# A recurrence followed by two gated MLPs: the two fp16 copies of each unit move from ScalarE to VectorE after the first four chunks

## Chip, cores and metric

The kernel runs on one core of one Trainium2 chip. The metric is the device time of one execution in microseconds (us); lower is better. Engine names are those of the profile: PE is TensorE (PEld its weight loads), DVE is VectorE, ACT is ScalarE, POOL is GpSimd, SP is SyncE, which here only issues DMAs.

## What is computed

The inputs of the recurrence have shape 4 x 8 x 768 x 40 (batch, heads, sequence, head size). Each of the 32 batch-head pairs carries a 40 x 40 state through 768 steps, and the output of a step is read before the state is updated. The 3072 x 320 result goes through two MLPs, the second of them gated.

```python
for t in range(S):
    y[:, :, t] = einsum('bhd,bhde->bhe', rt, state)
    Sa = einsum('bhde,bhe->bhd', state, at)
    state = state * wt[:, :, None, :] - einsum('bhd,bhe->bhde', Sa, bt) + einsum('bhd,bhe->bhde', vt, kt)
h = x @ w_in                      # 320 -> 2048
g = where(h >= 1, h, where(h <= -1, 0, (h + 1)**2 / 4))
x = g @ w_out                     # 2048 -> 320
out = (silu(x @ w_gate) * (x @ w_val)) @ w_out2   # 320 -> 1536 -> 320
```

## The kernel before, in words

**Chunks and units.** The sequence is cut into 12 chunks of 64 steps. Within a chunk the steps are solved together by matrix products and one triangular inverse, so that the state passes only from chunk to chunk. A unit is one chunk of one batch entry (8 heads); there are 4 units in a chunk and 48 in all, numbered n = 4c + j. Every fp32 operand of a matmul is kept as two fp16 parts, a high part and the rest, side by side in one tile.

**Stages.** `decay_tasks` (L664) builds running products of w and their reciprocals, for four chunks at a time. `p_tasks` (L788) prepares a unit: it scales a, r, k and b, splits them (tiles `ars`, `kbs`), turns them by a DMA transpose (`art`, `kbT`) and multiplies them (`lkt`, `l21`, and L to memory). `inv_tasks` (L885) solves the triangular system of a chunk on DVE in 31 steps of two operations (L915, L920). `m_tasks` (L973) is the part of a unit that depends on the state of the chunk before. `in1`, `in2` and `outp` (L1196, L1211, L1225) are the MLPs, on 256 rows (one chunk) at a time; their matmuls are at L1170 and L1234.

**What m_tasks does with a unit.** ACT loads v scaled (L994), casts it to the fp16 tile `vh` (L1018), and POOL writes the rest to `vss` (`split`, L539). A copy at L1026 writes `vh` twice into the first 64 rows of `vss` (64 x 640 values). PE multiplies (L1038). Then, for each of two half chunks: ACT writes two fp16 copies of the result (L1062), DVE the rest (L541, called from L1066), PE multiplies by the inverse (`mm_sa`, L1048), ACT and DVE split that into rows of `vss` (L1073, L541); between the halves PE runs `mm_c` (L1054). When `vss` is full, a DMA transpose turns it (`vsT`, L771), and a second copy, at L1098, puts both fp16 parts of all 128 rows of `vss` (128 x 640 values) beside the weights of the unit's output in tile `wt`. PE multiplies `vsT` (L1106), DVE masks it (L1109), ACT and DVE split it into the other part of `wt` (L1113, L539), and PE computes output and new state (L1127). DVE and ACT then scale and split the state (L1134 to L1146), which DMAs carry to where the next chunk reads it (L1148, L1152). The last chunk has no second copy, as it makes no state.

**Which engine makes the two copies.** Line L1025 chooses an operation, an engine and a cost for both: below chunk `VO` ACT's copy, from `VO` on DVE's. `VO` is 12 before the change, so ACT makes all 48 copies of L1026 and all 44 of L1098.

**What sets the order.** Nothing is issued in the order of the source. Each piece of work is a task with an engine, a cost, the results it reads, the buffers it uses and a first priority `p`. `Plan.forward` (L64) is a list scheduler run at build time: it starts on each engine the ready task of lowest priority number, and models buffers, DMA and PE's slower clock. A task marked `lk`, and every POOL task, keeps DVE and POOL apart: it is taken to begin its work only after the last such task of the other engine. `Plan.backward` goes over the same tasks from the end and gives new priorities; `run` (L301) alternates the two up to eight times and keeps the shortest plan. On each engine the tasks are then issued in that plan's order, and on the chip each engine works through its list in order.

**First priorities.** `m0(n)` (L1268) is the due time of a unit, from `PER` (one chunk) less `LEAD`. `decay_tasks`, `p_tasks`, `inv_tasks` and `m_tasks` get `m0` less leads of their own; `BP`, `BI`, `BM` and `BD` are extra leads of chunk 0 (of its p, inv and m tasks and of the first decay group), `P1` and `M1` those of chunk 1, and `DP` sets the second half of a decay group behind the first. The MLP tasks of chunk c are due at `PER` x c and on, whatever `LEAD` is.

Of the kernel before, what the change touches and what calls it, by code (L numbers as in the profile page):

```python
# [322 lines left out]
def tile_recurrence__then__gated_mlps(  # L323
# [35 lines left out]
    ARP = range(1, 12)  # L359
    XSP = range(12)  # L360
    NH = 1
    VO = 12
    WSP = True
    NW1 = 14
    NLO = 2
# [141 lines left out]
    def c_s(n):  # L507
        return 0.08 + n * 0.86e-3
# [464 lines left out]
    def m_tasks(n, p):  # L973
# [23 lines left out]
        if j % 2 == 0:  # L997
# [26 lines left out]
          r=[(key, "vh")], w=[(key, "vl")], use=V + VH + VS, p=p - 1)  # L1024
        copy, eng, cost = (s_.copy, "ACT", c_s(2 * HD)) if c < VO else (v_.tensor_copy, "DVE", 0.24)  # L1025
        T(eng, cost, lk=eng == "DVE", emit=lambda: copy(  # L1026
# [235 lines left out]
                    out=out[r0:r0 + C, :], in_=o()[64 * q:64 * q + 64]),  # L1262
                    r=[(ok, tt, 1)], w=[("out", c)], use=[("u", uk)], p=p, dma=0.31)

    PER, LEAD, PLEAD, DLEAD, WLEAD, ILEAD, WSTEP, LPRI, LSTEP, BP, BI, BM, DP, BD, P1, M1 = 69.67, 10.07, 94.28, 203.97, -34.92, 128.76, 0.3, 29.05, 2.22, -0.71, 2.76, 0.74, 10.0, 113.83, 18.78, 5.0
    SUP = PER / B

    def m0(n):  # L1268
# [112 lines left out]
```

## Time and profile before

| what | value |
|---|---|
| median of 3 runs (range) | 1157.68 us (1153.25 to 1157.78) |
| the profiled execution's own time | 1155.31 us |
| span of its profile, first to last instruction | 1153.6 us |
| mean granted clock of TensorE, share of full speed | 0.972 |
| PE busy | 910.4 us |
| ACT busy | 866.0 us |
| DVE busy | 755.0 us |
| POOL busy | 569.0 us |

The durations in this document come from the one profiled execution; 1.7 us of its time lie outside the span. Busy time is the time in which an engine has an instruction under way. In a table by stretches each engine has its busy time and, in brackets, its number of instructions, followed by the granted clock and the DMA engines' busy share. A line "A <- B" in a table of waits is idle time of engine A ahead of an instruction, ended by B: total, number of times, longest. In a table of groups the part after the bar is busy time and mean duration, then the idle time ahead of the group's instructions and what ended it. In the view of one line or tile, durations in ns are given as smallest, median and largest, then the first and the last start.

### The profile page before, as it was taken

What the parts mean: (1) busy time and instruction counts of PE and PEld (TensorE: products, weight loads), DVE (VectorE), ACT (ScalarE), POOL (GpSimd) and SP (SyncE); (2) the same over time, 40 slices, a digit from 0 to 9 for tenths busy, and PEclk for the clock granted to TensorE, in tenths of its full rate; (3) what the DMA queues carried; (4) which work ended last, traced back from release to release, by engine and by line L of the source; (5) the groups of instructions that cost most, each with busy time, mean ns of one, the idle gap of its engine ahead of it and who ended that gap; (6) DMA issues with size and microseconds to landing.
All of it is one profiled execution on the core that took longest, in us unless ns stands there. A gap on an engine that the chain in (4) does not pass through costs nothing. (4 is left out here: it accounts for less than half of the span.)

```text
span 1153.6 us, 29900 instructions
## 1 busy us (share of the span) xinstructions
PE 910.4 (79%) x11328; PEld 745.1 (65%) x11328; DVE 755.0 (65%) x1830; ACT 866.0 (75%) x1628; POOL 569.0 (49%) x756
## 2 busy tenths in 40 slices
PE   0131246744789899989999899999999999999998
PEld 0131235533567777777777787787777777888886
DVE  7778796886879487585765856856758457442211
ACT  2595687876996998988979979788798796763422
POOL 5689634533566536545554545545545433322321
PEclk9999999766899999999999999999999999999999
DMA  9988699669979888787977877799667534321000
GB/s 212 240 200 169 182 149 159 147 116 197 195 145 152 122 124 143 134 129 126 147 121 126 134 123 128 127 134 140 103 130 129 101 75 76 60 44 32 4 15 23
DMA packets 560948, 144.63 MB, mean 125 GB/s; under 512 B 537140, under 2 KB 544820, under 8 KB 560804
## 3 DMA queue, kind: packets, MB, share of 16 engines
q1 hardware_dynamic: 523036, 135.08, 64.8%
q10 hardware_dynamic: 37768, 7.66, 4.3%
q8 instruction: 88, 1.44, 0.6%
q14 instruction: 56, 0.46, 0.2%
HBM read 74.87 MB, written 18.14 MB: 81 GB/s over the span
## 5 line engine op out<-in xcount | busy, mean ns | idle before, releaser
L539 POOL TENSOR_TENSOR mx<-mx 128x512 f16<-128x512 f32 x168 | 194.7, 1161 | 271.8 <-ACT mx L1190 252.1
L1234 PE MATMUL po<-wo,mx 128*128 128x320 f16 x2016 | 314.3, 302 | 3.9 <-DVE mx L541 2.5
L1234 PEld LDWEIGHTS <-mx 128*128 128x128 f16 x2016 | 191.1, 98 | 72.9 <-DVE mx L541 2.8
L1170 PE MATMUL ph<-mx,w 128*128 128x256 f16 x1536 | 194.0, 278 | 17.4 <-DMA mx<-x 10.1
L1170 PEld LDWEIGHTS <-w 128*128 128x128 f16 x1536 | 147.6, 99 | 41.7 <-issue 18.4
L1170 PE MATMUL ph<-x2t,wv 128*128 128x256 f16 x1152 | 141.3, 272 | 4.9 <-DVE mx L1220 3.2
L1170 PE MATMUL ph<-x2t,wg 128*128 128x256 f16 x1152 | 140.9, 273 | 2.3 <-ACT mx L1216 2.2
L1190 ACT CAST mx<-mx 128x512 f16<-128x512 f32 x168 | 102.9, 615 | 48.1 <-DVE mx L1220 30.1
L1206 DVE SCALAR_TENSOR_TENSOR mx<-ph,mx 128x512 f32<-128x512 f32 x96 | 66.2, 690 | 94.6 <-ACT mx L1203 94.2
L1170 PEld LDWEIGHTS <-wv 128*128 128x128 f16 x1152 | 110.4, 98 | 20.0 <-issue 6.5
L1170 PEld LDWEIGHTS <-wg 128*128 128x128 f16 x1152 | 109.8, 98 | 17.7 <-issue 2.9
L920 DVE TENSOR_TENSOR pg<-pg,ub 128x126 f32<-128x126 f32 (+22 forms) x372 | 96.4, 259 | 9.8
L915 DVE SCALAR_TENSOR_TENSOR ub<-ub,pg 128x126 f32<-128x126 f32 (+22 forms) x372 | 92.4, 248 | 14.5 <-DMA ub<-lsd 4.5
L1220 DVE SCALAR_TENSOR_TENSOR mx<-ph,mx 128x512 f32<-128x512 f32 x72 | 49.4, 686 | 71.9 <-PE ph L1170 69.0
L1062 ACT ACTIVATE xs<-px 32x320 f16<-32x320 f32 x176 | 75.0, 426 | 11.6 <-PE px L1054 6.1
L545 POOL TENSOR_TENSOR ldp<-ldp 128x320 f32<-128x320 f32 (+1 forms) x90 | 76.6, 864 | 11.8 <-ACT ldp L822 5.5
L1073 ACT ACTIVATE vss<-px 32x640 f16<-32x640 f32 x88 | 61.1, 695 | 12.3 <-PE px L1048 10.3
L1048 PEld LDWEIGHTS <-tt 96*32 96x32 f16 x768 | 28.5, 95 | 64.4 <-issue 45.2
L541 DVE SCALAR_TENSOR_TENSOR xs<-px,xs 32x320 f16<-32x320 f32 x88 | 42.6, 484 | 39.7 <-ACT xs L1062 37.3
L1202 ACT ACTIVATE mx<-ph 128x512 f32<-128x512 f32 x96 | 57.0, 594 | 12.6 <-PE ph L1170 10.5
L539 POOL TENSOR_TENSOR vss<-ldv,vh 128x320 f16<-128x320 f32 x48 | 38.5, 801 | 56.5 <-ACT vh L1018 25.0
L541 DVE SCALAR_TENSOR_TENSOR vss<-px,vss 32x320 f16<-32x320 f32 x88 | 43.4, 493 | 30.0 <-ACT vss L1073 24.8
(226 smaller groups left out, 1713.9 us busy)
## 6 DMA issues: line engine op xcount, KB each, us to landing
ldv<-in_v_dram SPq DMA_DIRECT2D x88, 80.0 KB
ub<-lsd SPq DMA_DIRECT2D x22, 256.0 KB
wo<-in_moe_w_out_dram SPq DMA_DIRECT2D x17, 320.0 KB
ldp<-was SPq DMA_DIRECT2D x23, 160.0 KB
out_dram<-mx SPq DMA_DIRECT2D x46, 80.0 KB
wo<-in_moe_w_in_dram SPq DMA_DIRECT2D x7, 512.0 KB
ldp<-in_b_dram SPq DMA_DIRECT2D x22, 160.0 KB
ldp<-wks SPq DMA_DIRECT2D x22, 160.0 KB
```

The source lines that it names most:

```text
L539: e.tensor_tensor(out=out, in0=x, in1=hi, op=ALU.subtract)
L541: e.scalar_tensor_tensor(out=out, in0=x, scalar=scale, in1=hi, op0=ALU.mult, op1=ALU.subtract)
L545: e.tensor_tensor(out=out, in0=x, in1=y, op=ALU.mult)
L915: v_.scalar_tensor_tensor(out=t, in0=L()[:, j, j + 1:].unsqueeze(1).to_broadcast([128, nm, ni]), scalar=-(2.0**-10), in1=m[:, 0:nm, j:j + ...
L920: v_.tensor_tensor(out=m[:, 0:nm, j + 1:], in0=m[:, 0:nm, j + 1:], in1=t, op=ALU.add)
L1062: s_.activation(out=xs[32 * i:32 * i + 32], in_=px[32 * hf:32 * hf + 32], func=AF.Copy, scale=-(2.0**-10))
L1073: s_.activation(out=hi2(G("vss", key)[z]), in_=two(hd(G("px", key))[z]), func=AF.Copy, scale=2.0**-8)
L1170: t_.matmul(out=ps, lhsT=wts[:, wi, fs], rhs=xT[:, xi, :], start=(i == 0), stop=(i == len(plan) - 1))
L1190: T("ACT", c_s(512), lambda: s_.copy(out=G("g", key)[:, 0], in_=u2(key)), r=[(key, "u")], w=[(key, "gh")], use=U + GG, p=p)
L1202: s_.activation(out=u2(key), in_=ps2(key), func=AF.Relu, scale=2.0**-8, bias=1.0)
L1206: T("DVE", c_v(512, True), lambda: v_.scalar_tensor_tensor(out=u2(key), in0=ps2(key), scalar=2.0**8, in1=u2(key), op0=ALU.max, op1=ALU.min ...
L1234: t_.matmul(out=ps, lhsT=g[:, x, f, 128 * tt:128 * tt + 128], rhs=wo[:, 2 * i + f, y, :], start=(i == 0 and f == 0 and m == 0), stop=(i == ...
```

## The change

`VO` becomes 4: the copies at L1026 and L1098 are ACT's in chunks 0 to 3 and DVE's (`tensor_copy`) in chunks 4 to 11. Each DVE copy is given a cost of 0.24 to plan with, and the mark `lk`. Six of the planner's first-priority numbers change as well: `LEAD`, `BI`, `BM`, `DP`, `BD` and `M1`.

```diff
-    VO = 12
+    VO = 4
...
-    PER, LEAD, PLEAD, DLEAD, WLEAD, ILEAD, WSTEP, LPRI, LSTEP, BP, BI, BM, DP, BD, P1, M1 = 69.67, 10.07, 94.28, 203.97, -34.92, 128.76, 0.3, 29.05, 2.22, -0.71, 2.76, 0.74, 10.0, 113.83, 18.78, 5.0
+    PER, LEAD, PLEAD, DLEAD, WLEAD, ILEAD, WSTEP, LPRI, LSTEP, BP, BI, BM, DP, BD, P1, M1 = 69.67, 13.46, 94.28, 203.97, -34.92, 128.76, 0.3, 29.05, 2.22, -0.71, -1.04, 2.57, 15.51, 135.59, 18.78, 2.07
```

## Rows read from the trace of the kernel before

**Rows 1.** The page, busy time of each engine over the span.
```profile
span 1153.6 us, 29900 instructions
PE 910.4 (79%) x11328; PEld 745.1 (65%) x11328; DVE 755.0 (65%) x1830; ACT 866.0 (75%) x1628; POOL 569.0 (49%) x756
```

**Rows 2.** Table by stretches, four stages of the span.
```profile
core 0: us, PE busy (x) PEld busy (x) DVE busy (x) ACT busy (x) POOL busy (x), PEclk, DMA share, GB/s
0.00:180.00 180.00, 41.51 (x616) 35.67 (x617) 144.76 (x399) 114.07 (x197) 124.04 (x243) 1.00 0.88 189
180.00:420.00 240.00, 175.47 (x2193) 138.06 (x2193) 180.31 (x396) 195.89 (x373) 120.30 (x144) 0.87 0.84 153
420.00:1020.00 600.00, 563.91 (x7300) 464.03 (x7300) 402.75 (x993) 507.46 (x970) 290.75 (x337) 1.00 0.72 119
1020.00:1154.00 134.00, 129.49 (x1223) 107.34 (x1222) 27.23 (x43) 48.57 (x91) 33.93 (x34) 0.99 0.11 21
```

**Rows 3.** Waits of PE, from 420 to 1020 us.
```profile
PE px L1048 <- DVE xs L541: 11.8, 15, 1.4
PE px L1054 <- DVE vss L541: 4.5, 8, 1.6
PE pg L1127 <- DVE wt L539: 4.1, 10, 1.1
PE ph L1170 <- DVE mx L1220: 2.8, 3, 1.7
PE ph L1170 <- DVE mx L1206: 2.5, 4, 1.0
PE ph L1170 <- ACT mx L1216: 2.2, 3, 0.8
PE pg L1106 <- DMA vsT<-vss: 1.2, 1, 1.2
...
PE po L1234 <- POOL mx L539: 0.3, 1, 0.3
```

**Rows 4.** Waits of DVE, from 420 to 1020 us.
```profile
DVE mx L1206 <- ACT mx L1203: 56.0, 50, 4.7
DVE xs L541 <- ACT xs L1062: 26.4, 32, 2.6
DVE vss L541 <- ACT vss L1073: 20.5, 21, 2.4
```

**Rows 5.** Lines L1026 and L1098, the copies of chunks 4 and later.
```profile
L1026 ACT COPY vss<-vh x32: 708/724/729, 429.8 to 1016.3; 64x640 f16<-64x640 f16 x32
L1098 ACT COPY wt<-vss x28: 707/724/727, 473.4 to 968.5; 128x640 f16<-128x640 f16 x28
```

**Rows 6.** Lines L718 and L714, copies on DVE in the decay stage.
```profile
L718 DVE COPY wg<-wv x3: 176/184/500, 22.2 to 124.0; 128x40 f32<-128x40 f32 x3
L714 DVE COPY wv<-wg x3: 195/268/802, 10.5 to 108.7; 128x80 f32<-128x80 f32 x3
```

**Rows 7.** Timeline, the longest copy of L714 and POOL beside it.
```profile
8.71 3.96 POOL L1321 MEMSET l<- 128x704 f16 x6
10.53 0.80 DVE L714 COPY wv<-wg 128x80 f32<-128x80 f32 x1
```

**Rows 8.** Line L539 on DVE, the same subtraction with and without POOL busy.
```profile
L539 DVE TENSOR_TENSOR kbs<-ldp,kbs x2: 1145/1150/1154, 48.9 to 50.0; 128x320 f16<-128x320 f32 x2
...
L539 DVE TENSOR_TENSOR ars<-ldp,ars x1: 636/636/636, 48.4 to 48.4; 128x320 f16<-128x320 f32 x1
```

**Rows 9.** Line L545 on POOL, one shape.
```profile
L545 POOL TENSOR_TENSOR wg<-wg x62: 343/352/601, 36.6 to 114.8; 128x80 f32<-128x80 f32 x62
```

**Rows 10.** Waits of ACT, from 420 to 1020 us.
```profile
ACT vss L1026 <- DMA vsT<-vss: 4.0, 3, 2.2
```

**Rows 11.** Groups of PE, from 180 to 420 us.
```profile
L1170 PE MATMUL ph<-mx,w 128*128 128x256 f16 x384 | 52.8, 293 | 16.1 <-DMA mx<-x 9.8 <-DVE mx L1206 6.1 <-POOL w L539 0.2
...
L1048 PE MATMUL px<-xs,tt 96*32 96x40 f16 x184 | 8.7, 184 | 17.0 <-DVE xs L541 12.7 <-DMA tt<-tsd 4.3
```

## The prediction, made before the changed kernel ran

> **What bounds the kernel now.** I began with the busy time of each engine over the span [rows 1]. PE leads with 79%, but that is a mean over unlike stages, so I cut the span into four stretches [rows 2]. Up to 180 us PE has hardly any work. From 180 to 420 us it is busy 175.5 of 240 us, at a granted clock of 0.87. From 420 to 1020 us it is busy 563.9 of 600 us, 94%, at full clock (the upper level, 2.4 GHz), and from 1020 us to the end 129.5 of 134 us. All copies that the change moves, those of chunks 4 and later, ran between 429.8 and 1017 us [rows 5]. The third stretch therefore decides, and what can be won in it is PE's idle time: 600 - 563.9 = 36.1 us.
>
> What ends these idle times? In the waits of PE [rows 3] six lines hold 27.9 us (11.8 + 4.5 + 4.1 + 2.8 + 2.5 + 2.2): five end with a DVE operation and one with an ACT operation. POOL ends 0.3 us. In the waits of DVE [rows 4] the two subtractions for which PE waits longest (xs and vss at L541) themselves waited 26.4 and 20.5 us for ACT's half of the same split. So PE is the bound, and what makes it stop is mostly a chain ACT, then DVE, then PE in the recurrence. In this stretch ACT is busy 507.5 us (85%), DVE 402.8 us (67%), POOL 290.8 us (48%) [rows 2]. Work is taken from the fuller of the two engines of that chain and given to the emptier.
>
> **Step 1, what leaves ACT.** There are 32 copies at L1026 and 28 at L1098, with a median of 0.724 us [rows 5]: 60 x 0.72 = 43.2 us. ACT falls from 507.5 to 464.3 us, 77%. None of the 60 ends a wait of PE in the listing, so none stands on PE's path by itself; the gain comes only from what was queued behind them on ACT.
>
> **Step 2, what comes to DVE.** No fp16 copy on DVE is in the trace. The nearest rows are the fp32 copies [rows 6]: undisturbed, 40 values a row took 176 ns and 80 took 195, which is 0.48 ns a value over a fixed 156 ns. At that price per value 640 values would take 0.46 us; if two fp16 values go in the place of one fp32 value, 0.31 us. I take 0.31, since each row is the same number of bytes as 320 fp32 values. The ends are 0.18 us (the shortest such copy) and 1.15 us (the longest simple DVE operation on 128 rows, [rows 8]).
>
> The Trainium skill, "VectorE: DVE Perf Modes", section "The TRN2 errata", gives 58 cycles + values / 4 at 0.96 GHz for such a copy, an estimate of 0.23 us; with the wait of step 3 that would be 26 us on DVE and the sum below would gain 0.4 us more.
>
> **Step 3, the wait that comes with it.** A DVE copy of 80 values took 0.80 us, where 0.195 is its undisturbed time, while a run of POOL memsets was under way [rows 6, 7]. A subtraction with both inputs in SBUF took 1.15 us beside POOL and 0.64 without [rows 8]. POOL suffers too: one of its products took 601 ns, with a median of 352 [rows 9]. So a copy that meets POOL waits for about the rest of its instruction. POOL is busy 48% of the stretch with 337 instructions of 0.86 us on average [rows 2]; half of 0.86 us, 48% of the time, is 0.21 us a copy. With it a copy holds DVE 0.52 us, 60 of them 31.2 us: DVE goes from 402.8 to 434.0 us, 72%. POOL's own stretching, at most 60 x 0.25 = 15 us, is hidden by its idle 309 us, as PE hardly waits for POOL; without that cover it would be paid by the second MLP matmul at L1234.
>
> The copy at L1026 also brings its own waits: three times ACT stood in front of it until the transpose of the unit before had freed vss, 4.0 us, 2.2 at the longest [rows 10]. On DVE those stand ahead of the subtractions at L541, for which PE waits. The copy at L1098 loses a hop between engines instead, for it follows a subtraction that DVE itself has made. No DMA is issued by either copy; the transposes on SP's queue wait for DVE's copy in place of ACT's, which in both cases is ready before the last half of vss. I cost these points (the wait for vss, the hop saved, the transpose) at nothing; without that cover the transpose would start up to 0.5 us late.
>
> **Step 4, what that does to PE.** I take waiting in a chain of two engines as proportional to load over spare time, an estimate from the stretch's own figures [rows 2]. Before: ACT 507.5 / 92.5 = 5.48, DVE 402.8 / 197.2 = 2.04, together 7.52. After: ACT 464.3 / 135.7 = 3.42, DVE 434.0 / 166.0 = 2.61, together 6.03, or 0.80 of it. One fifth of 27.9 us is **5.5 us** gained. With DVE's price at its ends the same sum gives 7.0 us (0.18 us a copy) and 1.6 us (1.15 us a copy); with DVE free of charge 7.6 us.
>
> **Step 5, the priority numbers.** LEAD puts every task of the recurrence 3.39 us sooner against the MLP tasks; chunk 0's m tasks come 5.2 us sooner, chunk 1's 0.5, chunk 0's inverse 0.4 us later, the first decay group 25 us sooner, although it already opens the span. In the second stretch PE waits 16.1 us in front of the first MLP and 17.0 in front of mm_sa, 9.8 and 12.7 of it for the recurrence's results [rows 11], so sooner is the right side. The most is the lead itself, 3.4 us; the worst is the same again lost, when the plan, which is drawn anew, lays the start less well. I take half of the gain, **1.7 us**. The stretches before 420 us and after 1020 us hold no copy that moves (but the last of L1026), and I cost them at nothing else.
>
> **Sum.** 5.5 + 1.7 = 7.2 us. Against the profiled execution's own time that is 1155.3 - 7.2 = 1148.1 us. That execution lies 2.4 us below the median of the runs shown; put on the median, 1157.7 - 7.2 = **1150.5 us**.
>
> **Rivals.** *The copies stand in the chain (slower).* DVE works in order. If a copy that waits for POOL is placed ahead of a subtraction at L541 or the mask at L1109, the next matmul of the recurrence is late by the whole 0.52 us. For it: DVE and PE wait there already [rows 3, 4], and the slowing beside POOL is in the trace [rows 7, 8]. Against it: both copies can run at leisure, and the planner is told of the lock. It decides from 15 copies on (7.6 / 0.52), a quarter of the 60. With half of them on the path it costs 30 x 0.52 = 15.6 us, less 7.6 us: 8.0 us slower, 1165.7 us.
>
> The Trainium skill, "Advanced Engine Details and Errata", section "VectorE Performance Modes", states that VectorE's second SBUF port is shared with GpSimd and that two-port vector instructions and GpSimd block each other. By that rule this change pays on every copy that meets POOL. The trace agrees in the rows of the decay stage (0.80 us against 0.195).
>
> *ACT's load was hidden.* PE is busy at 94% already, and waits in a list that was planned need not shrink with an engine's load; the new plan packs the list as tightly as before and stops PE elsewhere. For it: no copy ends a PE wait. Against it: the six waits lie behind ACT and DVE. Time: 1157.7 us, give or take 3.
>
> *The new order of the start is what counts.* From 180 to 420 us PE idles 64.5 us [rows 2], more than in the stretch with the copies. If the other priority numbers save 15% of that, 9.7 us come on top of the forecast: 1140.8 us. For it: the waits named in step 5. Against it: DVE is busy 75% and DMA 84% there, and leads of a few us do not remove work from either.
>
> **How the numbers follow.** Forecast 0.53, its own range 1145 to 1155 us; copies in the chain 0.14; hidden 0.21; start 0.12. A measurement of this kernel can tell about 0.5%, 5.8 us, from no change: faster is below 1151.9 us, slower above 1163.5. The forecast, close to that line, gives 0.39 to faster and 0.14 to the same; the start's 0.12 is faster, the hidden case's 0.21 the same; the chain case gives 0.02 to the same and 0.12 to slower. That makes 0.51, 0.37 and 0.12. The range runs from 1136 to 1166 us: it takes in the forecast with both ends of DVE's price, the hidden case, and the middle of the two outer cases.
>
> **What would show it.** Right: 60 COPY instructions on DVE at L1026 and L1098 with a smallest duration near 0.31 us and a spread up to about 1.2; ACT's busy time down by about 43 us, DVE's up by 19 to 31; PE's idle time in the stretch that corresponds to 420 to 1020 us down from 36 to about 30 us, with fewer waits behind xs and vss. Wrong: new waits of PE behind DVE at L1048, L1054 or L1127 that are longer than before, or DVE idle ahead of its copies for POOL (the chain case); the same 36 us of PE idle under other names (hidden); or a difference that is already there when the first copy moves, at about 430 us (start).

## The result and the profile after

| | before | after |
|---|---|---|
| median, 6 runs each (range) | 1157.38 us (1153.25 to 1158.51) | 1164.12 us (1159.55 to 1166.68) |
| the profiled execution's own time / span | 1155.31 / 1153.6 us | 1164.93 / 1163.2 us |

The ratio after to before is 1.0063, with a 95% interval of 1.0044 to 1.0081. The change makes the kernel slower by 0.63%, some 7 us; the forecast was 7 us faster. Below, 0.1% is 1.16 us.

The busy times of the changed kernel, which answer to [rows 1]:

```profile
span 1163.2 us, 29953 instructions
PE 913.3 (79%) x11328; PEld 744.3 (64%) x11328; DVE 779.6 (67%) x1890; ACT 830.2 (71%) x1568; POOL 570.9 (49%) x756
```

Exactly 60 instructions went from ACT to DVE. ACT's busy time fell by 35.8 us and DVE's rose by 24.6. Both are less than the sum of the copies' durations (43.2 us on ACT, 34.7 on DVE), because neighbouring instructions overlap and busy time counts an overlap once. The table by stretches, as in [rows 2]:

```profile
core 0: us, PE busy (x) PEld busy (x) DVE busy (x) ACT busy (x) POOL busy (x), PEclk, DMA share, GB/s
0.00:180.00 180.00, 39.35 (x617) 33.97 (x618) 142.57 (x397) 113.40 (x196) 123.27 (x243) 0.69 0.86 188
180.00:420.00 240.00, 177.14 (x2213) 138.43 (x2213) 183.41 (x410) 198.29 (x377) 120.85 (x143) 0.85 0.80 155
420.00:1020.00 600.00, 557.74 (x7165) 456.99 (x7163) 421.14 (x1034) 462.52 (x891) 288.87 (x334) 0.99 0.75 117
1020.00:1164.00 144.00, 139.08 (x1342) 114.91 (x1338) 32.52 (x52) 56.02 (x106) 37.90 (x38) 1.00 0.10 23
```

Read PE's instruction counts. At 420 us PE had done 617 + 2213 = 2830 instructions, before 2809: the start lost nothing. From 420 to 1020 us it did 7165, before 7300, and its idle time rose from 36.1 to 42.3 us. The loss lies in the stretch with the moved copies, as does the relief: ACT is 45 us less busy there. The waits of PE in it, as in [rows 3]:

```profile
PE px L1048 <- DVE xs L541: 9.8, 16, 1.7
PE pg L1127 <- DVE wt L539: 6.9, 10, 2.7
PE px L1048 <- DMA tt<-tsd: 4.5, 3, 2.6
PE ph L1170 <- DVE mx L1220: 4.1, 5, 1.4
PE pg L1106 <- DMA vsT<-vss: 3.9, 3, 3.4
PE pg L1106 <- DVE lkt L876: 2.1, 6, 0.7
PE px L1054 <- DVE vss L541: 2.1, 7, 0.4
...
```

The two waits that were to shrink did: xs from 11.8 to 9.8 us, vss from 4.5 to 2.1. Others took their place: wt (4.1 before), the sign that the prediction gave for the copies standing in the chain, and two that end with a DMA, tt (0.9 before) and vsT (1.2).

The copies on DVE, one line of the program each:

```profile
L1026 DVE COPY vss<-vh x32: 307/473/2995, 423.7 to 1022.9; 64x640 f16<-64x640 f16 x32
...
L1098 DVE COPY wt<-vss x28: 307/329/1194, 466.7 to 970.5; 128x640 f16<-128x640 f16 x28
```

Undisturbed, a copy took 0.307 us. The longest took 3.0. The timeline around it (start, duration in us, engine, line):

```profile
473.63 0.79 POOL L539 TENSOR_TENSOR ars<-ldp,ars 128x320 f16<-128x320 f32 x1
...
474.29 3.00 DVE L1026 COPY vss<-vh 64x640 f16<-64x640 f16 x1
...
474.38 0.78 POOL L539 TENSOR_TENSOR vss<-ldv,vh 128x320 f16<-128x320 f32 x1
...
475.13 1.15 POOL L539 TENSOR_TENSOR mx<-mx 128x512 f16<-128x512 f32 x1
...
476.25 0.85 POOL L545 TENSOR_TENSOR ldp<-ldp 128x320 f32<-128x320 f32 x1
...
477.31 0.70 DVE L1109 TENSOR_TENSOR pg<-pg,mask 128x512 f32<-128x512 f32 x1
...
478.05 0.59 ACT L1113 CAST wt<-pg 128x512 f16<-128x512 f32 x1 [3.67 <-DVE pg L1109]
...
478.68 0.10 PEld L1127 LDWEIGHTS <-wt 128*128 128x128 f16 x1 [2.28 <-ACT wt L1113]
```

POOL had four instructions back to back, and the copy ended at 477.29 us, 0.2 us after the last of them (477.10). Behind it in DVE's list stood the mask at L1109; ACT's cast waited 3.67 us for that, and PE's weight load 2.28 us for the cast. This is the chain of the slower rival, from POOL to PE. Over all 60 the trace shows the same: the 11 copies with no POOL instruction beside them took 307 to 329 ns, and every longer one had at least one beside it; in the run with DVE copies in the old order, below, 18 met none, and took 307 to 328.

### The profile page after: what moved, and what is told of

Its sections match the earlier page's. It is cut to its first block, busy times and chain, and to the rows that moved or that the text cites. A ratio compares the mean times of both kernels' runs of the same rounds, so it can differ in the third digit from the quotient of the medians.

```text
span 1163.2 us, 29953 instructions
## 1 busy us (share of the span) xinstructions
PE 913.3 (79%) x11328; PEld 744.3 (64%) x11328; DVE 779.6 (67%) x1890; ACT 830.2 (71%) x1568; POOL 570.9 (49%) x756
## 4 chain that ended last, share of the span: by engine, by line
PE 27%; DVE 22%; ACT 16%; DMA 8%; issue 7%; SPq 3%; POOL 1%; ACTq 1%; DVEq 0%; POOLq 0%
PE ph L1170 14%; PE po L1234 10%; DVE pg L920 4%; DVE ub L915 4%; ACT xs L1062 3%; DMA ub<-lsd 2%; ACT mx L1202 2%; ACT vss L1073 2%; ACT mx L1190 1%; DVE mx L1220 1%; DVE vss L541 1%; DVE xs L541 1%; PE pg L1127 1%; ACT gf L860 1%; DVE pf L1158 1%
## 5 line engine op out<-in xcount | busy, mean ns | idle before, releaser
L539 POOL TENSOR_TENSOR mx<-mx 128x512 f16<-128x512 f32 x168 | 194.7, 1162 | 257.1 <-ACT mx L1190 233.6
L1170 PE MATMUL ph<-mx,w 128*128 128x256 f16 x1536 | 191.1, 277 | 19.9 <-DMA mx<-x 13.8
L545 POOL TENSOR_TENSOR ldp<-ldp 64x320 f32<-64x320 f32 (+1 forms) x90 | 77.0, 865 | 8.9 <-ACT ldp L822 4.7
L1202 ACT ACTIVATE mx<-ph 128x512 f32<-128x512 f32 x96 | 57.2, 596 | 22.0 <-PE ph L1170 14.6
L539 POOL TENSOR_TENSOR x<-pf,x 64x320 f16<-64x320 f32 x48 | 37.9, 790 | 70.9 <-ACT x L956 57.0
L1073 ACT ACTIVATE vss<-px 32x640 f16<-32x640 f32 x88 | 61.1, 695 | 12.5 <-PE px L1048 10.7
L1216 ACT ACTIVATE mx<-ph 128x512 f32<-128x512 f32 x72 | 43.0, 597 | 30.2 <-PE ph L1170 26.8
L1203 ACT ACTIVATE mx<-mx 128x512 f32<-128x512 f32 x96 | 60.5, 630 | 3.1
```

The lines of the kernel that those rows point to most:

```text
L539: e.tensor_tensor(out=out, in0=x, in1=hi, op=ALU.subtract)
L545: e.tensor_tensor(out=out, in0=x, in1=y, op=ALU.mult)
L1073: s_.activation(out=hi2(G("vss", key)[z]), in_=two(hd(G("px", key))[z]), func=AF.Copy, scale=2.0**-8)
L1170: t_.matmul(out=ps, lhsT=wts[:, wi, fs], rhs=xT[:, xi, :], start=(i == 0), stop=(i == len(plan) - 1))
L1202: s_.activation(out=u2(key), in_=ps2(key), func=AF.Relu, scale=2.0**-8, bias=1.0)
```

## The experiments

Every plan is drawn anew when a cost, an engine or a priority changes, so a comparison of two plans mixes two things. Most experiments therefore hold a plan and exchange only the instruction that is issued in the place of the 60 copies. Line numbers after L1025 are one or two higher in these kernels. Each ratio is to the old kernel run beside it on the same chip; a difference of two rows carries the intervals of both, 0.2 to 0.3% together.

| order of the tasks | copies of chunks 4 to 11 | ratio (95% interval) |
|---|---|---|
| old | ACT (the old kernel) | 1 |
| old | left out | 0.9951 (0.9936 to 0.9967) |
| old | POOL | 0.9958 (0.9941 to 0.9975) |
| old | DVE memset in their place | 1.0033 (1.0020 to 1.0046) |
| old | DVE | 1.0082 (1.0059 to 1.0105) |
| changed | left out | 0.9984 (0.9972 to 0.9996) |
| changed | POOL | 1.0010 (0.9996 to 1.0024) |
| changed | DVE memset in their place | 1.0022 (1.0005 to 1.0040) |
| changed | DVE (the changed kernel) | 1.0063 (1.0044 to 1.0081) |
| changed | ACT | 1.0193 (1.0171 to 1.0215) |
| VO = 4, old numbers | left out | 0.9991 (0.9979 to 1.0004) |
| VO = 4, old numbers | DVE | 1.0061 (1.0043 to 1.0078) |
| new numbers, VO = 12 | left out | 1.0009 (0.9991 to 1.0027) |
| new numbers, VO = 12 | ACT | 1.0086 (1.0067 to 1.0104) |
| planned with POOL copies, old numbers | POOL | 1.0039 (1.0026 to 1.0051) |
| LEAD 10.7 alone | ACT | 1.0039 (1.0025 to 1.0053) |
| LEAD 9.7 alone | ACT | 1.0156 (1.0134 to 1.0178) |
| LEAD 13.46 alone | ACT | 1.0090 (1.0073 to 1.0106) |

**Two orders, three ways with the copies.** The edits stand behind line L1025, after engine and cost have been set for the plan.

```diff
# changed order, copies on ACT
+        copy = s_.copy
# old order, copies on DVE
+        copy = s_.copy if c < 4 else v_.tensor_copy
# old order, and changed order: no copies from chunk 4 on
+        if c >= 4:
+            copy = lambda out, in_: None
```

> The order of all tasks is the changed kernel's, as planned with the copies on DVE; only the engine that executes the 60 copies is ACT again. Lock theory (the DVE copies that wait for POOL hold up the recurrence, and that is the loss): the 34.7 us of DVE time go, and the time falls from 1164 to 1157 us or below. Order theory (the loss lies in the order that the new plan gives to everything else): the time stays at 1164 us or rises by up to 8 us, since this order leaves no room on ACT for the copies.

> The order of all tasks is the old kernel's, as planned with the copies on ACT; only the engine that executes the copies of chunks 4 to 11 is DVE. Lock theory: DVE copies cost what the changed kernel lost, 1157 becomes 1163 to 1168 us. Order theory: the engine matters little, 1154 to 1159 us. The sum of the prediction without the priority numbers: 1152 us.

> The changed kernel's order, with the 60 copies of chunks 4 to 11 left out (those parts of vss and wt keep what chunks 0 to 3 left there). It is the whole price of the DVE copies in this order. Lock theory: 1153 to 1157 us. Order theory: 1160 to 1164 us, still slower than the old kernel with all its copies.

> The old kernel's order, with the 60 copies of chunks 4 to 11 left out. It is the most that taking them off ACT can give in this order. If the relief of ACT reaches PE as predicted: about 7.6 us, 1150 us. If the load of ACT was hidden: 1155 to 1158 us.

In the old order, copies on ACT cost 0.49% over none, copies on DVE 1.31%. In the changed order DVE copies cost 0.79% and ACT copies 2.1%. So for ACT and DVE an order has room for the copies where it was planned to have them, and in the other order ACT's cost four times as much and DVE's 1.7 times; a fair comparison takes each kind in its own order. Neither theory is right alone: the changed order without any copy is 0.33% slower than the old one without (0.9984 to 0.9951), and the DVE copies add 0.79%. The two prices depend on each other: with DVE copies in both, the changed order is not slower than the old one (1.0063 and 1.0082). The stretch from 420 to 1020 us of the old order without copies, and then with DVE copies:

```profile
420.00:1020.00 600.00, 568.03 (x7376) 468.91 (x7375) 405.24 (x1000) 474.51 (x917) 292.71 (x339) 1.00 0.71 119
```

```profile
420.00:1020.00 600.00, 557.86 (x7197) 459.13 (x7196) 427.27 (x1046) 464.69 (x899) 288.64 (x334) 1.00 0.70 119
```

With the copies DVE, the third engine, is 22 us busier and PE, the first, is idle 42.1 us in place of 32.0.

**Time on DVE, or waiting?** A memset of zeros over the same cells has no input to fetch.

```diff
+        if c >= 4:
+            copy = lambda out, in_: v_.memset(out, 0.0)
```

> The old kernel's order, and in the place of the 60 copies of chunks 4 to 11 a VectorE memset of the same cells (the copies are left out, zeros stand in their place). A memset reads nothing; by the memset rows of the trace it should hold DVE for about 0.35 us, as long as an undisturbed copy (0.31). Lock theory: with no input to fetch it does not wait for POOL, and most of the 15 us that DVE copies cost against no copies goes: 1149 to 1154 us, durations all near 0.35 us. Theory of mere occupation of DVE: 1158 to 1163 us, as with the copies on DVE.

> The changed kernel's order, with a VectorE memset of the same cells in the place of each of its 60 DVE copies (the copies are left out). In this order DVE copies cost 0.79% (about 9 us) against none. If waiting for POOL is most of that price: 0 to 3 us above the run without copies, that is 0.998 to 1.001 of the old kernel. If mere occupation of DVE is most of it, as in the old order, where memsets cost 0.8% and copies 1.3%: 1.002 to 1.005 of the old kernel.

The two forms in the old order, first the copies, then the memsets:

```profile
L1027 DVE COPY vss<-vh x32: 307/321/1280, 430.9 to 1022.2; 64x640 f16<-64x640 f16 x32
...
L1099 DVE COPY wt<-vss x28: 307/608/1308, 474.3 to 975.0; 128x640 f16<-128x640 f16 x28
```

```profile
L1027 DVE MEMSET vss<- x32: 325/325/325, 430.7 to 1018.1; 64x320 uint32 x32
L1027 DVE MEMSET wt<- x28: 325/325/325, 474.1 to 971.2; 128x320 uint32 x28
```

The memsets all took 325 ns, beside POOL or not: as long as an undisturbed copy, with no waiting at all. They cost 0.82% in the old order, where copies cost 1.31, and 0.38% in the changed order, where copies cost 0.79. So about a half of what the copies cost, or somewhat more, is DVE's plain time, and the rest is mostly the waiting for POOL. A memset also skips the wait for the copy's own input, which is small (1.5 us in front of L1026 behind vh, in the changed kernel).

**POOL's copies.** Here the copies are POOL's, which has the most idle time.

```diff
+        copy = s_.copy if c < 4 else p_.tensor_copy
```

> The old kernel's order, with the copies of chunks 4 to 11 executed by POOL. No DVE instruction waits for POOL for their sake, and ACT is relieved as in the change. Lock theory: between no copies (1149 us) and the old kernel (1154 in that comparison), if POOL's idle half hides 60 copies of about 0.7 us. If what matters is that the copies stand in a list planned for another engine: 1160 us or more.

> The changed kernel's order, with the copies of chunks 4 to 11 executed by POOL. Theory from the old order (POOL hides them, what DVE copies cost is DVE's time and its waits): as without copies, 0.998 to 1.001 of the old kernel. Theory that copies on an engine other than the planned one always cost (ACT in this order: 2.1%): 1.006 or more.

In the old order this is 0.42% faster than the old kernel and 1.05% faster than the changed one; it is the best version of this study, and not to be told from leaving the copies out (0.9958 and 0.9951). POOL's copies take 0.71 and 0.72 us, and PE does not feel them. Its stretch from 420 to 1020 us, POOL being the fifth engine:

```profile
420.00:1020.00 600.00, 568.03 (x7360) 467.31 (x7358) 403.01 (x991) 472.02 (x913) 331.02 (x397) 1.00 0.72 119
```

PE is busy as long as without copies, with POOL at 55%. In the changed order POOL's copies cost 0.26%.

**The parts of the change, each with a plan of its own.**

```diff
# copies alone
-    VO = 12
+    VO = 4
# numbers alone: the new PER, LEAD, ... line, VO stays 12
# POOL's copies planned
-    VO = 12
+    VO = 4
-        copy, eng, cost = ... else (v_.tensor_copy, "DVE", 0.24)
+        copy, eng, cost = ... else (p_.tensor_copy, "Pool", 0.72)
```

> Only the first part of the change: VO is 4, the priority numbers are the old ones, and the plan is drawn anew. Lock theory: the DVE copies cost about 9 us as in the changed kernel, the relief gives about 5: 1157 to 1165 us. Order theory with the numbers at fault: 1150 to 1154 us.

> Only the second part of the change: the new priority numbers with all copies on ACT, the plan drawn anew. Lock theory: without DVE copies the new numbers are worth at most some 4 us either way, 1150 to 1162 us. Order theory with the numbers at fault: 1160 to 1166 us.

> The order planned with VO at 4 and the old priority numbers, with the copies of chunks 4 to 11 left out. It tells what this order is worth without the copies, beside 0.995 for the old order and 0.998 for the changed one. If the new numbers make the changed order worse: 0.994 to 0.996 here, and DVE copies cost 1.1% in it. If any order planned with DVE copies is as bad: 0.997 to 1.000.

> VO at 4 and the old priority numbers, but the copies of chunks 4 to 11 are POOL's in the plan as well as on the chip, at a cost of 0.72 as POOL's copies took in the old order. Lock theory: at least as good as in the old order, 0.992 to 0.996 of the old kernel. Order theory (a new plan is a new draw, worth some tenths of a per cent either way): 0.990 to 1.004.

Each part alone is as slow as the whole (1.0061, 1.0086, 1.0063), so the parts do not add. Once the copies are DVE's, the new numbers make no difference that could be measured: 1.0061 with the old ones and 1.0063 with the new, and 0.9991 and 0.9984 without copies. Planning with POOL's copies is 0.8% worse than putting them into the old order. Three different reasons for a new plan, and each lost: I then asked what a new plan is worth for no reason at all.

**Redrawing the old plan.** Only LEAD is altered, from 10.07 to 10.7, then to 9.7, then to 13.46. Beside them, the order of all new numbers is run without the copies.

```diff
-    ... = 69.67, 10.07, 94.28, ...
+    ... = 69.67, 10.7, 94.28, ...
```

> The old kernel with LEAD at 10.7 in place of 10.07 and nothing else: all copies on ACT, the plan drawn anew. If a redrawn plan is by itself some tenths of a per cent worse than the old one: 1.002 to 1.009 of the old kernel. If it is the new numbers that are bad: 0.998 to 1.002.

> The old kernel with LEAD at 9.7 and nothing else, a second redrawn plan. Redrawing by itself: 1.002 to 1.009. The new numbers at fault: 0.998 to 1.002.

> The old kernel with LEAD at 13.46, the changed kernel's value, and nothing else. If the recurrence's earlier due times are what is bad in the new numbers: 1.006 to 1.010, as all six numbers together without the DVE copies (1.0086). If it is redrawing by itself: anywhere between 1.000 and 1.009, as the two small changes of LEAD.

> The order planned with the new numbers and all copies on ACT, with the copies of chunks 4 to 11 left out. If ACT's copies cost in this order what they cost in the old one (0.5%): 1.003 to 1.004 of the old kernel, and the order by itself is 0.8% worse. If copies on ACT cost more in it: 0.996 to 1.001.

Less than 0.7 us in one due time costs 0.39% or 1.56%. The redrawn plans with copies on ACT lie between 1.0039 and 1.0156, and the changed kernel lies among them. They are three and not four: the traces of LEAD at 13.46 and of all new numbers show the same instructions in the same order on every engine, so with the copies on ACT the other five numbers changed nothing, and the two ratios (1.0090 and 1.0086) are one plan measured twice. The loss is not special to the new numbers: every plan that was redrawn here lost against the old one, and a change that redraws it starts behind. How the old numbers were found is not on record; if they are the best of many that were tried, a loss is what a redraw would be expected to bring.

The planner itself saw the direction of this. `Plan.run` returns the length of the plan that it keeps, which is known as soon as a kernel is built: 1061.1 us for the old kernel and 1065.3 for the changed one. For VO = 4 with old numbers it is 1068.0, for the new numbers with VO = 12 1068.6, for POOL's copies 1061.4, and for LEAD at 10.7 and 9.7 1063.5 and 1081.7. No redrawn plan is shorter than the old one, and the longest plan gave the slowest of these runs, though the planned ratio misses the measured one by up to 0.4%.

In the order of the new numbers the copies on ACT cost 0.77%, about what DVE copies cost in theirs (0.79 and 0.70%).

## Why the prediction was wrong

It took the sum of two gains, 5.5 us from the relief and 1.7 us from the start. Measured along one path of the table: without ACT's copies -0.49% (-5.7 us), the redrawn order +0.33% (+3.8), DVE's time +0.38% (+4.4), the waits of its copies +0.41% (+4.7); together +0.63%. Each term carries 0.2 to 0.3% either way, and the split goes with the path: in the old order DVE's copies add 1.31% to the run without them, and the redrawn order then gives back 0.19%, which is within the noise. On either path the copies on DVE cost more than the relief of ACT was worth.

- **Step 1 (leaves ACT)** held: 60 copies, and their removal was worth 5.7 us, where step 4's figure with DVE free of charge was 7.6.
- **Steps 2 and 3 (what DVE gets)** held as durations: 0.307 us undisturbed where 0.31 was forecast, 34.7 us for all 60 where 31.2 was forecast, the wait for POOL included. The spread did not: up to about 1.2 us was expected, and the longest took 3.0. The Trainium skill's cycle table in "VectorE: DVE Perf Modes", section "The TRN2 errata", from which an estimate of 0.23 us was worked out, is below the measured 0.307; the section itself says that the row is too low for a single operation, and the measurement decides. One reading behind step 3 was wrong, without weight in its sum: the subtraction of 0.64 us that stands in [rows 8] as the one without POOL ran beside it (start and duration in us, before):

```profile
48.07 0.60 POOL L545 TENSOR_TENSOR wg<-wg 128x80 f32<-128x80 f32 x1
...
48.38 0.64 DVE L539 TENSOR_TENSOR ars<-ldp,ars 128x320 f16<-128x320 f32 x1
```

- **Step 4 failed, and with it the sum.** It said that waiting goes with load over spare time, engine by engine, which let 31 us on DVE cost PE only 7.6 - 5.5 = 2.1 us. They cost 9.1 us (0.79%) in the changed order and 15 us (1.31%) in the old one. An engine at 67% is not the cheaper one when PE waits for it last: five of PE's six longest waits ended with DVE [rows 3]. The formula knew the load of an engine but not its place in the chain, and it spread the waits for POOL evenly, though one copy that meets four POOL instructions holds the recurrence for 3 us.
- **Step 5 failed too.** It gave the new priority numbers +1.7 us and at worst -3.4. With the copies on DVE they are worth nothing that could be measured (1.0061 and 1.0063), and alone they cost 0.86%. The sum had no term for what a redrawn plan costs in the stretch with the copies, and moving them redraws it by itself: without copies that order is 0.40% slower than the old one with the old numbers and 0.33%, 3.8 us, with the new. A redraw for a trifle costs 0.4 to 1.6%, 5 to 18 us. This range should have been in the forecast's range: a list scheduler that picks the best of eight plans does not answer to a small change with a small change.
- **The slower rival** named the right mechanism and nearly the time (1165.7 us), and the reason the prediction gave against it, that the planner is told of the lock, did not hold: in an order drawn with the lock in its model the copies still took 15 us more than 60 undisturbed memsets (34.7 - 60 x 0.325). But along the path above the waiting is only about 0.4% of it, DVE's plain time as much, and the order 0.3%.
- **The hidden rival** fell: taking the load off ACT does shorten the run. **The start rival** fell: at 420 us the two kernels stand level.

The Trainium skill's rule in "Advanced Engine Details and Errata", section "VectorE Performance Modes", that two-port VectorE instructions and GpSimd block each other, is borne out by the copies here (0.307 to 2.995 us), and the Trainium skill's "GPSIMD Engine Reference", section "Key points", which limits the contention to two-port instructions and those with two SBUF inputs, by the memsets (325 ns, all of them).

What remains open: which feature of a redrawn order costs the 0.3 to 1.6%. In the changed kernel one place can be seen. From 952 to 972 us the timeline shows a transpose, PE's wait for it, and what followed:

```profile
953.26 1.29 SPq L771 DMA_TRANSPOSE vsT<-vss  x1
...
955.61 1.04 PE L1170 MATMUL ph<-x2t,wv 128*128 128x256 f16 x8
...
960.02 0.61 PE L1106 MATMUL pg<-lsp,vsT 120*128 120x64 f16 x8 [3.38 <-DMA vsT<-vss]
...
961.26 1.88 PE L1170 MATMUL ph<-x2t,wv 128*128 128x256 f16 x8
...
962.93 3.25 PE L1234 MATMUL po<-wo,mx 128*128 128x320 f16 x12
```

The transpose landed 6.7 us after its issue, and PE, whose next instruction it was, stood for 3.4 us. The same 8 matmuls of wv took 1.04 us before and 1.88 us after. The changed order without copies has the same hole (3.7 us); the order planned with VO at 4 and the old numbers has not, and is as slow. That place is a part of it at most, and it was not isolated. The longer DMA waits of the result's table belong to the order and not to the copies, for they stand in the changed order without copies as well, where the old order without copies has 0.8 and 1.2:

```profile
PE pg L1108 <- DMA vsT<-vss: 4.2, 3, 3.7
PE px L1050 <- DMA tt<-tsd: 4.0, 4, 1.5
```

They are not what the redrawn plans have in common: with the new numbers and VO = 12 these two are 0.9 and 0.8 us, and that kernel is 0.86% slower than the old one. Nor do the profiles show the order's 0.33% as idle time of PE in the stretch, which without copies is 30.2 us in the changed order and 32.0 in the old; over the span PE is busy for 913.1 us in the first and 910.7 in the second, with the same number of matmuls.

## What to carry to other kernels

Do not choose an engine by its busy share: ask for which engine the bound one waits last, and test by leaving the work out in a held order, which prices it before it is moved. Where a scheduler draws the order, hold the order to judge an engine, read the new plan's own length before the kernel runs, and redraw for nothing to learn the scatter; here that scatter (up to 1.6%) was larger than the effect looked for (0.5%). A VectorE copy from SBUF beside a busy GpSimd was not a 0.31 us instruction here but one of up to 3.0; on GpSimd itself the same copies cost nothing that could be measured in the old order.

## What was not expected of the hardware

The granted clock of the first 180 us was 1.00 in the profile before and 0.69 after, with the same work done in it, and it did not follow the kernel: the old order without copies also ran it at a mean of 0.69, and ended 5 us earlier. A mean clock over the whole span (0.972 before, 0.918 after) therefore told nothing of the time here. In the stretch that decides it was 1.00 before and 0.99 after, and the fall sits behind the hole shown above: 0.86 (between the two levels, 1.2 and 2.4 GHz) from 950 to 975 us.

```profile
950.00:975.00 25.00, 21.06 (x251) 16.57 (x251) 17.94 (x49) 16.22 (x36) 6.67 (x9) 0.86 0.72 91
```
